# The first table of a two-dimensional transform: loaded in pieces, on three queues, and twelve products of zeros

## Chip, cores and metric

The kernel runs on one core of one Trainium2 chip. The metric is the device time of one execution in microseconds (us), taken from outside the kernel. One core has a matrix engine (PE, with its weight loads listed as PEld), a vector engine (DVE), a scalar engine (ACT), GpSimd (POOL) and a queue-only engine (SP). DMAs are issued from SP, ACT and POOL.

## The reference

Two independent results are computed from 2048 x 576 inputs and set side by side. The first is an attention with 32 heads and a running memory. The second, the one the change is in, is a filter in the frequency domain:

```
X = rfft2(x)            # x is 1 x 2048 x 576
y = irfft2(X * (w_r + 1j*w_i), s=(2048, 576))
out = concatenate([attention(A_x, ...), y], axis=-1)
```

## The kernel before, in words

The program is one long hand-ordered sequence (a manual schedule): the forward transform of the filter, with the weights of the attention loaded beside it; then the projections of the attention, with the middle of the filter beside them; then the inverse transform; then the attention itself. Each engine runs its instructions in the order in which the code emits them.

All large products are done in a split form: an fp32 value is written as a high part in fp32r plus the rest, and high x high, high x low and low x high products are summed in PSUM. An fp32r tile has to be written by something that rounds: ScalarE, VectorE, or a DMA issued from POOL.

The forward transform (`forward`) works on 16 units of 128 sequence positions. For unit u:

- `load(u)` (L114, SP) fetches the rows `xin`, 384 KB, three buffers. `prep(u)` then has VectorE form sum and difference `eo` (L126, two instructions), ScalarE round them to the high part `eh` (L129, L130), and VectorE subtract to get the rest `el` (L133). For units 0 and 1 (`halves`) all this is done for the sum and the difference apart.
- `f1(u)` (L143) is the transform along the 576 columns: 14 products, 7 for each of the two outputs r = 0 (cosines) and r = 1 (sines), with the constant table `tab[:, high or low, r, chunk]` and the short `tab2`.
- `ev0` (L147, ScalarE) and `ev1` (L150, VectorE) take the result from PSUM as high part and rest, `X0` and `X1`.
- `c1(u)` (L163) is the transform along 128 positions: 12 products with the unit's own table `cfw` (`loadc`, L118, POOL), whose blocks are cosine, sine and negated sine, each in high and low. `evz` (L154, ScalarE) stores the result to `Z`.

A loop over u = 0 to 19 emits these in a fixed pipeline. Step u holds, in this order: `ev0(u-1)`, `evz(u-4)`, the first half of `prep(u+2)` (`eo`, `eh`), `ev1(u-1)`, one background instruction of the next stage (`pace`, L208, from step 7 on), the second half of `prep(u+2)` (`el`), `f1(u)`, `load(u+4)`, `c1(u-3)`, `loadc(u+1)`, and a piece of the projection weights (`load_w`: L420 load, L408 ScalarE, L410 VectorE). `prep(0)` and `prep(1)` stand ahead of the loop. So on VectorE a step is: `eo` of unit u+2, `X1` of unit u-1, background, `el` of unit u+2, weights. On ScalarE it is: `X0` of unit u-1, `Z` of unit u-4, `eh` of unit u+2, weights.

Ahead of the loop, POOL fetches the first table in three DMAs (L170: all of the high part, L172: all of the low part, L173: `tab2`) and the first four `cfw`; SP fetches `xin` of units 0 to 2 and the small constants `ident` and `bm` (L404).

Of the kernel before, what the change touches and what calls it, by code (L numbers as in the profile page):

```python
# [5 lines left out]
F32=mybir.dt.float32; F32R=mybir.dt.float32r  # L6
# [19 lines left out]
def tables():  # L26
# [26 lines left out]
    for s2 in range(16):  # L53
        ph=(16*s1*k1+s2*k1)%S
        a=2*np.pi*ph/S
        re=np.cos(a); im=-np.sin(a)
        im[(ph*2)%S==0]=0; re[(ph*4)%S==S]=0; re[(ph*4)%(2*S)==S]=0
        cf.append(np.concatenate([re,im,-im],1))
        ph=ph.T
        re=re.T; im=-im.T  # L60
        ci.append(np.concatenate([-im,re,im],1))
# [1 line left out]
    ci=np.stack(hilo(np.stack(ci)),1).transpose(0,2,1,3)  # L63
    w16=np.zeros((2,9),np.float32)
    return dict(ftab=fwd.reshape(128,-1),ftab2=fwt.reshape(128,-1),itab=inv.reshape(128,-1),itab2=ivt.reshape(128,-1),
                cfw=cf.reshape(16,128,768),civ=ci.reshape(16,128,768))

BORD=[(a,b) for b in range(4) for a in range(4)]

# [33 lines left out]
class FFT:  # L103
# [4 lines left out]
    def forward(s,xp,cp,pp,wl,xs,consts):  # L108
# [6 lines left out]
        def loadc(u):  # L115
            a,b=BORD[u]
            cw[u]=cp.tile([128,2,384],F32R,name="cfw",bufs=4)
            nc.gpsimd.dma_start(cw[u],io["cfw"][4*a+b].rearrange("p (h m) -> p h m",h=2))  # L118
        def prep(u,halves=False):

            x=xin.pop(u)
            eo=xp.tile([128,2,3,128],F32,name="eo",bufs=2)
            h=H[u%3]
            W=(slice(0,1),slice(1,2)) if halves else (slice(0,2),)
            for r,op in enumerate((OP.add,OP.subtract)):
                v.tensor_tensor(eo[:,r],x[:,0],x[:,1],op=op)  # L126
                if halves or r:
                    w=W[r] if halves else W[0]
                    nc.scalar.copy(h[:,w,:2],eo[:,w,:2])  # L129
                    nc.scalar.copy(h[64:97,w,2],eo[64:97,w,2])  # L130
            yield
            l=xp.tile([128,2,3,128],F32R,name="el",bufs=3)
            for w in W: v.tensor_tensor(l[:,w],eo[:,w],h[:,w].bitcast(F32),op=OP.subtract)  # L133
            eh[u],el[u]=h,l
            yield
        def f1(u):
            p=pp.tile([128,2,512],F32,name="f1",tag="f1")
            h,l=eh.pop(u),el.pop(u)
# [24 lines left out]
                        nc.tensor.matmul(p[:,r,:FP],cc[:,hl,k*128:(k+1)*128],x[i][:,q],start=n==0,stop=n==5)  # L163
                        n+=1
        H=[xp.tile([128,2,3,128],F32R,name=f"eh{i}",bufs=1) for i in range(3)]
        for h in H: nc.gpsimd.memset(h[:,:,2].bitcast(F32),0.0)
        load(0)
        tab=cp.tile([128,2,2,2,FP],F32R,name="ftab",bufs=1)
        tab2=cp.tile([128,2,FP],F32R,name="ftab2",bufs=1)
        nc.gpsimd.dma_start(tab[:,0],io["ftab"][:,:4*FP].rearrange("p (r c f) -> p r c f",r=2,c=2))  # L170
        late=consts()
        nc.gpsimd.dma_start(tab[:,1],io["ftab"][:,4*FP:].rearrange("p (r c f) -> p r c f",r=2,c=2))  # L172
        nc.gpsimd.dma_start(tab2,io["ftab2"].rearrange("p (r f) -> p r f",r=2))  # L173
        load(1); load(2); late()
        for u in range(2): loadc(u)
        p=[prep(u,True) for u in range(2)]
        for i in range(2):
            for x in p: next(x)
        load(3)
        s.pace=Pace(61+165+40)  # L180
        for u in range(20):
            p=prep(u+2) if u+2<16 else iter(())
            if 0<u<17: ev0(u-1)
            if 3<u: evz(u-4)
            if u%4==3 and u>6: s.pace.add(s.stage1((u-7)//4))
            next(p,None)
            if 0<u<17: ev1(u-1)
            if u<14: s.pace.take(1)
            next(p,None)
            if u<16: f1(u)  # L190
            if u+4<16: load(u+4)
            elif u<18: next(xs,None)
            if 2<u<19: c1(u-3)
            if 0<u<15: loadc(u+1)
            if 1<u: next(wl,None)
            if u>13: s.pace.take(2)
# [959 lines left out]
```

## Time and profile before

| what | value |
|---|---|
| three runs | 711.28, 709.81, 708.51 us; median 709.81 us |
| the profiled execution, whole | 709.86 us |
| its span, first to last instruction | 708.2 us, so 1.66 us lie around it |
| busy in the span: PE / DVE / ACT / POOL | 678.8 / 544.8 / 455.8 / 194.6 us |
| first wait of PE for the first table | until 9.6 us |
| granted clock of the core | 0.999 |

In the groups and timelines a row gives start, length, engine, line, operation, `out<-in` by the names of the program, shapes, a count, and in square brackets the idle time ahead of it with the engine or DMA that ended it. Products are pipelined, so the pitch from one start to the next says more than the length of one. In a table by stretches the columns are, engine by engine, busy time and number of instructions, then the granted clock of PE, the busy share of the DMA engines, and GB/s.

### The profile page before, as it was taken

To read this page: it belongs to the slowest core of one execution; us is meant where nothing else is said; L and a number is where in the kernel's file an instruction comes from. 1 tells how busy PE (TensorE), PEld (TensorE's weight loads), DVE (VectorE), ACT (ScalarE), POOL (GpSimd) and SP (SyncE) were. 2 spreads that over 40 slices of the span, in tenths; PEclk is the share of its full clock that TensorE was granted. 3 is DMA by queue.
4 is the path that set the end of the run, shared out by engine and by line. 5 is a ranking of instruction groups with operands and counts; after the bars stand their busy time and mean duration, and the time that the engine had idled before them with its cause. 6 is when DMAs were issued, how large, how long until landed. Compare 5 with 4: busy or idle time off the path is not lost.

```text
span 708.2 us, 14408 instructions
## 1 busy us (share of the span) xinstructions
PE 678.8 (96%) x4991; PEld 501.3 (71%) x4991; DVE 544.8 (77%) x1258; ACT 455.8 (64%) x1004; POOL 194.6 (27%) x392
## 2 busy tenths in 40 slices
PE   4999999999999999999999899999999999998997
PEld 3999769879779879998954454445566445663587
DVE  4899969899699789797787787988657876567533
ACT  3777796585686484544388777777656776567421
POOL 3111000100200102665135333444233752235310
PEclk9999999999999999999999999999999999999999
DMA  9897355666384679999338976976766766442151
GB/s 328 256 305 202 115 141 187 186 185 202 100 250 156 178 196 311 202 240 267 100 114 210 190 163 143 207 182 167 154 129 181 182 166 154 92 122 65 29 164 74
DMA packets 71146, 123.80 MB, mean 175 GB/s; under 512 B 12184, under 2 KB 39174, under 8 KB 67482
## 3 DMA queue, kind: packets, MB, share of 16 engines
q1 hardware_dynamic: 64422, 106.89, 57.4%
q0 software_dynamic: 5632, 15.76, 8.2%
q8 instruction: 39, 0.64, 0.4%
q10 hardware_dynamic: 1020, 0.25, 0.2%
q14 instruction: 33, 0.27, 0.1%
HBM read 82.10 MB, written 39.81 MB: 172 GB/s over the span
## 4 chain that ended last, share of the span: by engine, by line
PE 68%; DMA 8%; ACT 4%; DVE 4%; POOL 2%; issue 2%; SPq 0%; ACTq 0%; DVEq 0%; POOLq 0%
PE pj L464 12%; PE pv L734 9%; PE s L656 9%; PE pjv L464 8%; PE po L877 6%; PE i L309 3%; PE i L298 3%; PE s L705 3%; PE s L709 2%; DMA yb<-yout 2%; PE pn L807 2%; PE s L669 2%; PE pm L532 2%; PE s L714 2%; DMA Ks<-qkD 1%
## 5 line engine op out<-in xcount | busy, mean ns | idle before, releaser
L664 DVE CUSTOM_DVE_ANT_0 junk<-s,x 128x512 bf16<-128x512 f32 x248 | 137.0, 552 | 58.0 <-PE s L656 52.6
L719 POOL TENSOR_SCALAR_AFFINE_SELECT P<-P 128x512 f32<-128x512 f32 (+2 forms) x132 | 78.5, 626 | 112.9 <-ACT P L706 104.1
L670 DVE TENSOR_REDUCE mx<-s 128x4 f32<-128x512 f32 x128 | 87.7, 685 | 5.6 <-PE s L669 3.7
L706 ACT ACTIVATE P<-s 128x512 f32<-128x512 f32 x128 | 77.7, 607 | 10.8 <-PE s L705 3.8
L734 PE MATMUL pv<-P,vs 128*32 128x512 f32 (+3 forms) x1024 | 82.5, 439 | 0.1
L715 ACT ACTIVATE P<-s 128x256 f32<-128x256 f32 x128 | 49.8, 389 | 46.1 <-PE s L714 45.7
L711 ACT ACTIVATE P<-s 128x512 f32<-128x512 f32 x128 | 77.4, 605 | 2.4 <-PE s L710 2.2
L656 PE MATMUL s<-Ks,Qs 108*128 108x384 bf16 (+3 forms) x256 | 69.1, 301 | 1.5 <-DMA ux<-uD 1.0
L734 PEld LDWEIGHTS pv<-P,vs 128*32 128x32 f32 x1024 | 26.9, 109 | 45.3 <-issue 35.1
L464 PE MATMUL pj<-x,wqkh 128*128 128x512 f32 x162 | 56.5, 409 | 0.0
L208 DVE TENSOR_TENSOR Z<-t,t 128x290 f32<-128x290 f32 (+1 forms) x96 | 48.4, 553 | 0.1
L656 PEld LDWEIGHTS <-Qs 108*128 108x128 bf16 x320 | 31.5, 98 | 23.5 <-issue 12.1
L208 DVE TENSOR_TENSOR t<-Z 128x580 f32<-128x580 f32 x64 | 46.1, 755 | 0.0
L669 PE MATMUL s<-tri,idb 128*128 128x128 bf16 x256 | 43.0, 219 | 0.0
L522 POOL MEMSET vt<- 128x32 f32 x16 | 2.3, 162 | 141.3 <-PE pm L532 119.5
L298 PE MATMUL i<-civ,Y 128*128 128x256 f32 (+1 forms) x288 | 39.3, 289 | 0.2 <-POOL Y L283 0.2
L298 PEld LDWEIGHTS i<-civ,Y 128*128 128x128 f32 (+1 forms) x288 | 36.5, 181 | 1.0 <-POOL Y L283 0.4
L309 PE MATMUL i<-itab,T 128*128 128x290 f32 (+1 forms) x224 | 36.7, 306 | 0.5 <-DVE yout L317 0.4
L464 PE MATMUL pj<-x,wqkl 128*128 128x512 f32 x90 | 35.6, 395 | 0.0
L464 PE MATMUL pj<-xh,wqkl 128*128 128x512 f32 x90 | 35.5, 395 | 0.0
L143 PE MATMUL f<-ftab,eh 128*128 128x290 f32 x128 | 25.3, 321 | 10.7 <-DMA ftab<-ftab 10.6
L464 PE MATMUL pj<-xh,wqkh 128*128 128x512 f32 x90 | 35.5, 395 | 0.0
(210 smaller groups left out, 1806.3 us busy)
## 6 DMA issues: line engine op xcount, KB each, us to landing
qkD<-sp SPq DMA_DIRECT2D x32, 384.0 KB
xin<-xb SPq DMA_DIRECT2D x16, 384.0 KB
cfw<-cfw POOLq DMA_DIRECT2D x16, 384.0 KB, 4.7
civ<-civ POOLq DMA_DIRECT2D x16, 384.0 KB, 9.0
vs<-vD SPq DMA_DIRECT2D x16, 330.0 KB
vD<-vt SPq DMA_DIRECT2D x16, 311.0 KB
W<-w SPq DMA_DIRECT2D x16, 290.0 KB
yb<-yout SPq DMA_DIRECT2D x16, 290.0 KB
```

Source lines behind the costliest of these rows:

```text
L208: v.tensor_tensor(o,a,b,op=op)
L298: nc.tensor.matmul(p[:m,k],Y[i][:,q,c*128:c*128+m],cc[:,hl,o:o+256],start=n==0,stop=n==5)
L309: nc.tensor.matmul(p,x,t,start=n==0,stop=n==6)
L464: s.nc.tensor.matmul(out,a,b,start=i==0,stop=i==len(L)-1)
L656: nc.tensor.matmul(out,Q[:108,h,128*i:128*i+128],K[:108,h,:128*(i+1)],start=True,stop=True)
L664: nc.vector.tensor_tensor_reduce(out=junk[:,:w],in0=src,in1=s.mask[:,512-w:],scale=1.0,scalar=-3.0e38, op0=OP.add,op1=OP.max,accum_out=s.m ...
L669: nc.tensor.matmul(pa[:,o+w-128:o+w],s.idb,s.tri,start=False,stop=True,skip_group_check=True)
L670: nc.vector.tensor_reduce(out=s.mx[k][:,hh],in_=pa.rearrange("p (b c) -> p b c",c=128),axis=mybir.AxisListType.X,op=OP.max)
L706: nc.scalar.activation(P[0][:,hh],p0,AF.Exp,scale=SC)
L711: nc.scalar.activation(P[1][:,hh],p1,AF.Exp,scale=SC)
L719: nc.gpsimd.affine_select(out=x[:,r],in_=x[:,r],pattern=[[0,r.stop-r.start],[1,128]],compare_op=OP.is_ge,fill=0.0,base=0,channel_multiplie ...
L734: nc.tensor.matmul(s.pvt[32*hh:32*hh+32,128*j:],vt[:,j,19*h:19*h+32],mv[0][:,hh,mv[1]],start=j==0,stop=j>1,skip_group_check=True)
```

## The change

The first table is no longer loaded in three DMAs by POOL alone. It is cut into five pieces of 290 KB. Three of them (high r = 0, low r = 0, high r = 1) go as plain fp32 through the queues of ACT, SP and ACT into buffers of `cfw`, and ScalarE copies them into the fp32r table (`table(n)`, L180 of the changed kernel), between the roundings of the first units. POOL loads `tab2` and low r = 1. `prep` yields after each half, so that the first unit's cosine half is rounded first. The constants `ident` and `bm` move behind `load(3)`. The zeroing of `eh` moves from POOL to VectorE. Twelve products of a tile of zeros are put ahead of the loop on PE; their result is not used. The unit tables `cfw` are stored without the negated third (256 KB in place of 384 KB), and ScalarE makes that block by a copy with scale -1, one instruction per unit, two units before it is used.

```
-        cf.append(np.concatenate([re,im,-im],1))
+        cf.append(np.concatenate([re,im],1))
...
-            nc.gpsimd.dma_start(cw[u],io["cfw"][4*a+b].rearrange("p (h m) -> p h m",h=2))
+            nc.gpsimd.dma_start(cw[u][:,:,:256],io["cfw"][4*a+b].rearrange("p (h m) -> p h m",h=2))
...
-            yield
+                    yield
             l=xp.tile([128,2,3,128],F32R,name="el",bufs=3)
-            for w in W: v.tensor_tensor(l[:,w],eo[:,w],h[:,w].bitcast(F32),op=OP.subtract)
-            eh[u],el[u]=h,l
-            yield
+            for w in W:
+                v.tensor_tensor(l[:,w],eo[:,w],h[:,w].bitcast(F32),op=OP.subtract)
+                eh[u],el[u]=h,l
+                yield
...
-        for h in H: nc.gpsimd.memset(h[:,:,2].bitcast(F32),0.0)
+        z=xp.tile([128,512],BF,name="z",bufs=1)
+        v.memset(z,0.0)
+        for h in H: v.memset(h[:,:,2].bitcast(F32),0.0)
         load(0)
...
-        nc.gpsimd.dma_start(tab[:,0],io["ftab"][:,:4*FP].rearrange("p (r c f) -> p r c f",r=2,c=2))
+        nc.gpsimd.dma_start(tab2,io["ftab2"].rearrange("p (r f) -> p r f",r=2))
+        nc.gpsimd.dma_start(tab[:,1,1],io["ftab"][:,6*FP:].rearrange("p (c f) -> p c f",c=2))
         late=consts()
-        nc.gpsimd.dma_start(tab[:,1],io["ftab"][:,4*FP:].rearrange("p (r c f) -> p r c f",r=2,c=2))
-        nc.gpsimd.dma_start(tab2,io["ftab2"].rearrange("p (r f) -> p r f",r=2))
-        load(1); load(2); late()
+        raw=[]
+        for q,src in ((nc.scalar,io["ftab"][:,:2*FP]),(nc.sync,io["ftab"][:,4*FP:6*FP]),(nc.scalar,io["ftab"][:,2*FP:4*FP])):
+            x=cp.tile([128,2,384],F32,name="raw",tag="cfw",bufs=4)[:,:,:FP]; raw.append(x)
+            q.dma_start(x,src.rearrange("p (c f) -> p c f",c=2))
+        def table(n): nc.scalar.copy((tab[:,0,0],tab[:,1,0],tab[:,0,1])[n],raw[n])
+        load(1); load(2)
         for u in range(2): loadc(u)
         p=[prep(u,True) for u in range(2)]
-        for i in range(2):
-            for x in p: next(x)
-        load(3)
+        table(0); next(p[0]); table(1); next(p[0]); next(p[0]); table(2); next(p[0])
+        for x in p[1]: pass
+        load(3); late()
+        p=pp.tile([128,2,512],F32,name="c1",tag="c1")
+        for i in range(12): nc.tensor.matmul(p[:,0],z[:,:128],z,start=True,stop=True)
         s.pace=Pace(61+165+40)
         for u in range(20):
             p=prep(u+2) if u+2<16 else iter(())
             if 0<u<17: ev0(u-1)
             if 3<u: evz(u-4)
+            if 1<u<18: nc.scalar.activation(cw[u-2][:,:,256:],cw[u-2][:,:,128:256].bitcast(F32),AF.Copy,scale=-1.0)
```

The first place at which the order of instructions moves is the start of ScalarE's program (eh_112, eh_113 and eh_114 are the buffers of units 0, 1 and 2). Before:

```order
L129 ACT_TABLE_LOAD
L129 CAST eh_112<-eo 128x256
L130 CAST eh_112<-eo 33x128
L129 CAST eh_112<-eo 128x256
L130 CAST eh_112<-eo 33x128
L129 CAST eh_113<-eo 128x256
L130 CAST eh_113<-eo 33x128
```

With the change, on the same engine at the same place:

```order
L179 DMA raw<-ftab 128x2x290 x2
L180 ACT_TABLE_LOAD
L180 CAST ftab<-raw 128x580
L129 CAST eh_112<-eo 128x256
L130 CAST eh_112<-eo 33x128
L180 CAST ftab<-raw 128x580
L129 CAST eh_112<-eo 128x256
L130 CAST eh_112<-eo 33x128
L180 CAST ftab<-raw 128x580
L129 CAST eh_113<-eo 128x256
```

Two DMA issues and three copies now stand there, and unit 1's first rounding stands behind the third copy.

The second place is the start of SP's queue. Before, the three first units, the two small constants, and the fourth unit and those after it:

```order
L114 DMA xin<-xb 128x768 x3
L404 DMA ident<-ident 128x128
L404 DMA bm<-bm 126x133
L114 DMA xin<-xb 128x768 x4
L420 DMA raw<-wqk 128x576
```

With the change:

```order
L114 DMA xin<-xb 128x768
L179 DMA raw<-ftab 128x2x290
L114 DMA xin<-xb 128x768 x3
L414 DMA ident<-ident 128x128
L414 DMA bm<-bm 126x133
L114 DMA xin<-xb 128x768 x3
L430 DMA raw<-wqk 128x576
```

A piece of the table now stands between units 0 and 1, and the constants behind unit 3.

The third place is one step of the loop on ScalarE, u = 4: X of unit 3, Z of unit 0, the rounding of unit 6 and a piece of the weights. Before:

```order
L147 CAST X_293<-f_259 128x580
L154 COPY Z<-c_276 128x580
L129 CAST eh_112<-eo 128x2x256
L130 CAST eh_112<-eo 33x2x128
L408 CAST wqkh<-raw 128x576
```

With the change:

```order
L148 CAST X_318<-f_284 128x580
L155 COPY Z<-c_301 128x580
L194 ACTIVATE cfw<-cfw 128x2x128
L129 CAST eh_112<-eo 128x2x256
L130 CAST eh_112<-eo 33x2x128
L418 CAST wqkh<-raw 128x576
```

The negation stands ahead of the rounding that VectorE's `el` waits for.

2 lines of the change are left out of this document (1 added, 1 removed).

## The prediction

> **What bounds the kernel.** I read the page first, then the waits of PE, then the start of the program and the loop of the forward transform engine by engine.
>
> ```profile
> span 708.2 us, 14408 instructions
> PE   4999999999999999999999899999999999998997
> ```
>
> PE is busy nearly throughout; the one slice with a large hole is the first. The longest of PE's waits (total, times, longest):
>
> ```profile
> PE f L143 <- DMA ftab<-ftab: 10.6, 2, 9.6
> ```
>
> So 10.6 us of PE's time go to the first table, and one would expect a gain of several us. But an earlier start of PE is worth only what the engines that feed it can follow. The busy table by stretches (PE, PEld, DVE, ACT, POOL, clock, DMA share, GB/s):
>
> ```profile
> 0.00:5.00 5.00, 0.00 (x0) 0.00 (x0) 1.02 (x2) 1.69 (x2) 4.39 (x16) 1.00 0.57 198
> 5.00:10.00 5.00, 0.38 (x1) 0.41 (x2) 3.69 (x9) 2.39 (x7) 0.99 (x2) 1.00 1.05 343
> 35.00:40.00 5.00, 5.00 (x39) 5.00 (x38) 5.00 (x10) 3.07 (x7) 0.53 (x1) 1.00 0.96 322
> 50.00:55.00 5.00, 4.97 (x37) 4.73 (x36) 5.00 (x10) 3.14 (x6) 0.53 (x1) 1.00 0.88 266
> ```
>
> From 35 us on VectorE is busy all the time, and PE later gets through 37 products in 5 us where it had 39. The starts of units 9 and 10 on PE, and a line of the waits after 15 us:
>
> ```profile
> 40.73 0.69 PE L143 MATMUL f<-ftab,eh 128*128 128x290 f32 x4
> ...
> 44.35 0.81 PE L143 MATMUL f<-ftab,eh 128*128 128x290 f32 x4
> ```
>
> ```profile
> PEld f L143 <- DVE X L150: 1.2, 5, 0.3
> ```
>
> Unit 10 starts 3.62 us after unit 9, and five times PE waits for VectorE's X1, which frees the PSUM of `f1`. So the end of the forward transform hangs on VectorE's chain. That chain itself:
>
> ```profile
> 9.32 1.03 DVE L126 TENSOR_TENSOR eo<-xin 128x384 f32<-128x384 f32 x2 [1.18 <-DMA xin<-xb]
> 11.45 0.96 DVE L133 TENSOR_TENSOR el<-eo,eh 128x768 fp32r<-128x768 f32 x1 [1.11 <-ACT eh L130]
> 13.62 1.03 DVE L126 TENSOR_TENSOR eo<-xin 128x384 f32<-128x384 f32 x2 [1.21 <-DMA xin<-xb]
> 15.68 0.76 DVE L150 TENSOR_TENSOR X<-f,X 128x580 fp32r<-128x580 f32 x1 [1.03 <-ACT X L147]
> 16.75 0.96 DVE L133 TENSOR_TENSOR el<-eo,eh 128x768 fp32r<-128x768 f32 x1 [0.31 <-ACT eh L130]
> 17.63 1.02 DVE L126 TENSOR_TENSOR eo<-xin 128x384 f32<-128x384 f32 x2
> ...
> 20.70 1.02 DVE L126 TENSOR_TENSOR eo<-xin 128x384 f32<-128x384 f32 x2
> ...
> 43.54 0.75 DVE L150 TENSOR_TENSOR X<-f,X 128x580 fp32r<-128x580 f32 x1
> ```
>
> From unit 4's `eo` at 17.63 no step of it waits for PE or a DMA any more: it is 3.07 us to unit 5's, and on to 43.54 there is only the turn through ScalarE's rounding inside a step. The row at 43.54 is the X1 behind which PE starts unit 10 at 44.35. **Whatever the change does at the start counts by what it does to 17.63**, not by when PE begins. Behind the forward transform PE's digits are 9 nearly everywhere, so no gap would take up a shift; I carry a shift to the end whole.
>
> **The change part by part.** First, when does unit 4's `eo` come? Before, it hung on the first table: ScalarE's X of unit 0 waited for PE, and the rounding of unit 3 stood behind it.
>
> ```profile
> 4.58 0.41 ACT L129 CAST eh<-eo 128x256 fp32r<-128x256 f32 x1 [2.48 <-DVE eo L126]
> 5.01 0.29 ACT L130 CAST eh<-eo 33x128 fp32r<-33x128 f32 x1
> ...
> 15.01 0.64 ACT L147 CAST X<-f 128x580 fp32r<-128x580 f32 x1 [3.59 <-PE f L143]
> 15.67 0.62 ACT L129 CAST eh<-eo 128x512 fp32r<-128x512 f32 x1
> ```
>
> That wait goes, since unit 0's products will be through before unit 3's `eo`. What is late next is the arrival of unit 1: a piece of the table now stands ahead of it on SP, and two more run beside it on ACT's queue. From unit 1's landing the chain is: one `eo` half, 0.55; two pairs of roundings, 0.75 each (0.43 to the second, 0.29 for it and a hop); the last `el` half, 0.5, so 2.55 to unit 2's `eo`. From there 3.0 to unit 3's (2.13 from 9.32 to `el`, and 0.88 from an `el` to the next `eo`, as from 16.75 to 17.63), then one step of 3.07. Sum 8.6. ScalarE's third copy (0.64 by the 580 wide cast) runs while unit 1's `eo` is formed, if its piece lands no later than unit 1. So nothing is gained or lost if **unit 1 lands at 17.63 - 8.6 = 9.0 us**. Unit 3's own landing, 13.62 before, does not bind: two of the four unit tables no longer run ahead of it, and it has until 14.6.
>
> When does unit 1 land? Two stretches of the DMA view (1 to 2 and 2 to 3 us), the sizes, and the first uses:
>
> ```profile
> DMA packets 8, 0.02 MB, mean 25 GB/s; under 512 B 0, under 2 KB 0, under 8 KB 8
> DMA packets 94, 0.29 MB, mean 289 GB/s; under 512 B 0, under 2 KB 0, under 8 KB 94
> ```
>
> ```profile
> xin<-xb SPq DMA_DIRECT2D x16, 384.0 KB
> ftab<-ftab POOLq DMA_DIRECT2D x2, 580.0 KB, 8.2
> ```
>
> ```profile
> 3.98 2.15 DVE L126 TENSOR_TENSOR eo<-xin 128x384 f32<-128x384 f32 x4 [3.98 <-DMA xin<-xb]
> ...
> 9.62 0.82 PE L143 MATMUL f<-ftab,eh 128*128 128x290 f32 x2 [9.62 <-DMA ftab<-ftab]
> ```
>
> A unit is 0.393 MB and a piece, a quarter of 1160 KB, 0.297 MB. By 5 us 0.99 MB have come (198 GB/s), then 343 GB/s. Units 0 and 1 with the three plain pieces are 1.68 MB, there at 7.0 us; with POOL's two pieces all ahead, 2.27 MB, 8.7 us; with one of them 7.9. What is moved is usable later: unit 0's 0.393 MB are through at 3.3 us and used at 3.98, 0.7 later; three units and the first half of the table, 1.77 MB, are through at 7.3 and used at 9.62, 2.3 later. Bounds for unit 1: 7.7 and 11.0. I take 7.9 and 1.2, so 9.1: half of POOL's pieces, and a lag nearer to that of the same queue and size. **The start costs 0.1 us, with a gain of 1.3 and a loss of 2.0 as its ends.**
>
> The Trainium skill, DMA: Bandwidth & Descriptors, section Issuing engines are not separate DMA queues, speaks against the change: DMAs started by scalar, sync and gpsimd run on the same 16 engines and interleave. By that rule all 2.27 MB share the way, unit 1 would come at the late end, and the sum would be 711.9. The DMA share of 1.05 from 5 to 10 us agrees that no engine was spare there.
>
> Second, the twelve zero products and the earlier first product. The early products run at about half pace, though the clock column says 1.00:
>
> ```profile
> 13.07 1.17 PE L143 MATMUL f<-ftab,eh 128*128 128x290 f32 x4
> 14.04 0.93 PE L143 MATMUL f<-ftab,el 128*128 128x290 f32 x3
> ...
> 17.72 0.71 PE L143 MATMUL f<-ftab,eh 128*128 128x290 f32 x4
> 18.27 0.57 PE L143 MATMUL f<-ftab,el 128*128 128x290 f32 x3
> ```
>
> Four products take 0.97 us from start to start at 13.07 and 0.55 at 17.72, so 0.24 and 0.14 each; the 28 products of units 0 and 1 at the fast pace would save at most 2.8 us. That is under cover: VectorE wants units 0 and 1 only after unit 3's `eo`. I count 0, with 2.8 as the bound on the gain. The zero products themselves run in PE's empty first 9 us and cost nothing.
>
> The Trainium skill, TensorE: Matmul & The Clock Gate, Part 1, says that the array starts at half clock, is released by some 3.4 us of activity, and falls back after as long an idle stretch. The two pitches agree with it, the clock column does not show it; by the rule the zero products would buy 2.8 us on PE, a sum of 707.1 if PE set the end.
>
> Third, the negation on ScalarE: one 128 x 256 instruction per unit, 0.43 from start to start by the rounding at 4.58. It stands ahead of `eh`, where ScalarE idles:
>
> ```profile
> 39.89 0.62 ACT L129 CAST eh<-eo 128x512 fp32r<-128x512 f32 x1 [0.98 <-DVE eo L126]
> ```
>
> 0.98 us hide 0.43; I count 0. Without that cover each of the ten steps 4 to 13, those with a weight piece, would cost 0.43. For the last two units, whose products follow without an `f1` between, I count 0 too, with 0.43 each as the bound.
>
> Fourth, 128 KB less per unit table, 2.1 MB in all: the waits after 15 us name no DMA in the forward transform's loop, so 0 either way. The table loads of units 1 to 3 now wait for ScalarE's copies; behind them POOL has only further unit tables, used past 21 us. The zeroing on VectorE falls into its idle 3.98 us; the moved constants are used after the forward transform: 0.
>
> **Sum:** 709.86 (the span of 708.2 and 1.66 around it) + 0.1 = **710.0 us**; the profiled execution lies at the median of the three runs, 709.81.
>
> **Rivals.** (a) PE's start sets the end after all: then unit 2, at 17.72 on PE before, starts when its `el` is ready, 5.5 us behind unit 1's landing, at 14.6: 3.1 us gained, 706.7, and 705.5 if the five waits for X1 (1.2 us) go too. For it speaks the first slice of PE; against it, the row at 44.35. (b) Slower by transfers: unit 1 lands at 11.0, because POOL's and ACT's pieces share the DMA engines with SP and come through first; this decides from 9.0 us on, and its 2.0 us give 711.9. (c) Slower by the negation: if it waits for its table, or takes over 0.9 us, `eh` comes late in ten steps, and 0.43 each gives 714.2. Against it stands the idle 0.98. (d) The zero products do not speed PE up: then the 2.8 us stay, under cover, and it is 710.0 all the same, so (d) shares my forecast's chance.
>
> **How the numbers follow.** Forecast 0.55, (a) 0.16, (b) 0.18, (c) 0.11. The range goes down to 706.7 by (a), and up to 711.9 by (b) and 0.7 for the scatter between the runs, 712.6; left out are (c) and the far end of (a), some 0.19. Half a per cent is 3.5 us, about what a measurement of this kernel can tell from no change: faster than 706.3 is two thirds of (a), 0.10; slower than 713.4 nearly all of (c), 0.10; the rest is 0.80.
>
> **What would show it.** Right: unit 1's `eo` on VectorE at about 9 us, unit 4's at 17 to 18, the X1 ahead of unit 10 near 43.5, PE waiting for X1 from an earlier unit than 10, while PE's own first products come several us earlier and at 0.14. Wrong: unit 4's `eo` more than 2 us from 17.63; the idle time ahead of `eh` gone; products waiting for a negation; or a shift at 44.35 that doesn't arrive at the end.

## The result, and the profile after

| | before | with the change |
|---|---|---|
| median of the runs beside each other (22 each) | 709.59 us (706.68 to 713.31) | 711.76 us (709.25 to 716.56) |
| the profiled execution, whole / its span | 709.86 / 708.2 us | 711.22 / 709.5 us |
| granted clock of the profiled execution | 0.999 | 0.991 |

The ratio is 1.0036, with a 95% interval of 1.0023 to 1.0049, that is 2.6 us slower (1.6 to 3.5); the medians lie 2.2 us apart. 710.0 was forecast with a range of 706.7 to 712.6, so the time lies inside the range, and less than half a per cent from before, but the 0.1 us of the forecast is too little by about 2. The upper part of the range stood for a late landing of unit 1, which did not happen; that the time falls into it has other causes, which follow.

The head of the page of the changed kernel (span, and the slices of PE):

```profile
span 709.5 us, 14451 instructions
PE   7999999999999999999999999999999999998987
```

PE's first slice is busy to 7 tenths where it was 4, the zero products among them, as the change was meant to do. Nothing came of it. The start of VectorE shows the forecast chain, row by row:

```profile
8.68 1.03 DVE L126 TENSOR_TENSOR eo<-xin 128x384 f32<-128x384 f32 x2 [0.54 <-DMA xin<-xb]
...
14.61 1.02 DVE L126 TENSOR_TENSOR eo<-xin 128x384 f32<-128x384 f32 x2
15.54 0.76 DVE L151 TENSOR_TENSOR X<-f,X 128x580 fp32r<-128x580 f32 x1
16.80 0.96 DVE L134 TENSOR_TENSOR el<-eo,eh 128x768 fp32r<-128x768 f32 x1 [0.50 <-ACT eh L130]
17.67 1.02 DVE L126 TENSOR_TENSOR eo<-xin 128x384 f32<-128x384 f32 x2
```

Unit 1 is there for VectorE at 8.68 (9.1 was taken) and unit 4's `eo` comes at 17.67, against 17.63 before and a forecast of 17.7. PE on the other hand starts 3.6 us earlier (6.00 in place of 9.62) and has nothing left of it a few units on:

```profile
1.26 5.30 PE L188 MATMUL c<-z 128*128 128x512 bf16 x12 [1.26 <-DVE z L168]
6.00 1.51 PE L144 MATMUL f<-ftab,eh 128*128 128x290 f32 x4
...
8.51 0.40 PE L144 MATMUL f<-ftab,el 99*128 99x290 f32 x1 [0.74 <-DMA ftab<-ftab]
9.77 1.46 PE L144 MATMUL f<-ftab,eh 128*128 128x290 f32 x4 [0.86 <-ACT ftab L180]
...
16.35 0.81 PE L144 MATMUL f<-ftab,eh 128*128 128x290 f32 x4 [1.68 <-DVE X L151]
...
17.62 1.17 PE L144 MATMUL f<-ftab,eh 128*128 128x290 f32 x4
18.59 0.93 PE L144 MATMUL f<-ftab,el 128*128 128x290 f32 x3
...
21.91 1.79 PE L164 MATMUL c<-X,cfw 128*128 128x290 f32 x12
```

It waits for `tab2`, the short table that POOL loads (by the order of the program the product at 8.51 is the one that reads it; the trace leaves the number off the name), for ScalarE's copy of the third plain piece, and for unit 0's `X1` (the 15.54 on VectorE), and behind these waits its clock is at half again: four products take 0.97 us from 17.62 to 18.59. Now the clock column shows it (table by stretches, with the columns of the prediction):

```profile
10.00:13.60 3.60, 3.54 (x15) 3.30 (x15) 2.06 (x4) 1.94 (x6) 0.71 (x1) 0.54 1.29 362
...
17.00:20.40 3.40, 3.40 (x16) 3.14 (x15) 2.90 (x5) 2.42 (x5) 0.00 (x0) 0.52 0.70 223
```

The mean clocks of the two traces, 0.999 and 0.991, do not measure what the change lost here: before, units 0 and 1 ran at the same half pace (0.24 a product) while the column said 1.00.

The first c1 starts at 21.91, and unit 11 on PE at 48.33 where it was 48.16: the forward transform is as it was, within 0.2 us. Behind it stands a wait that the forecast did not have. The first product of the projections, before and with the change:

```profile
71.57 0.63 PE L464 MATMUL pj<-x,wqkh 128*128 128x512 f32 x2
```

```profile
72.63 0.74 PE L474 MATMUL pj<-x,wqkh 128*128 128x512 f32 x2 [0.73 <-ACT Z L155]
```

The product waits for the evacuation of unit 15's `Z` by ScalarE (71.93 to 72.57), and starts 1.06 us later than before. Before there is no wait. So three questions were open: where this wait comes from, where the rest of the loss comes from, and why 3.6 us on PE are worth nothing.

### The profile page after: what moved, and what is told of

Read it like the earlier page. It is cut to its first block, busy times and chain, and to the rows that moved or that the text cites. A ratio compares the mean times of both kernels' runs of the same rounds, so it can differ in the third digit from the quotient of the medians.

```text
span 709.5 us, 14451 instructions
## 1 busy us (share of the span) xinstructions
PE 685.9 (97%) x5003; PEld 505.1 (71%) x5003; DVE 546.3 (77%) x1262; ACT 462.4 (65%) x1023; POOL 195.5 (28%) x388
## 5 line engine op out<-in xcount | busy, mean ns | idle before, releaser
L680 DVE TENSOR_REDUCE mx<-s 128x4 f32<-128x512 f32 x128 | 87.7, 685 | 5.2 <-PE s L679 3.3
L474 PEld LDWEIGHTS pj<-x,wqkh 128*128 128x128 f32 x162 | 30.4, 188 | 8.2 <-ACT Z L155 1.0
```

The source lines that it names most:

```text
L474: s.nc.tensor.matmul(out,a,b,start=i==0,stop=i==len(L)-1)
L680: nc.vector.tensor_reduce(out=s.mx[k][:,hh],in_=pa.rearrange("p (b c) -> p b c",c=128),axis=mybir.AxisListType.X,op=OP.max)
```

## The experiments

All twelve ran in five rounds beside the kernel before. The table gives for each what the readings below use: unit 4's `eo` on VectorE, the first product of unit 2 on PE, the first projection product, and the ratio to the kernel before.

| kernel | unit 4's `eo` | unit 2 on PE | first projection | ratio (95%) |
|---|---|---|---|---|
| before | 17.63 | 17.72 | 71.57 | |
| the change | 17.67 | 16.35 | 72.63 | 1.0036 (1.0023 to 1.0049) |
| e1_again | 17.46 | 16.14 | 72.54 | 1.0032 (1.0014 to 1.0051) |
| e2_f1bank | 17.38 | 16.05 | 71.31 | 1.0021 (1.0004 to 1.0038) |
| e3_no_neg | 17.41 | 16.09 | 72.23 | 1.0026 (1.0008 to 1.0043) |
| e4_chain | 17.73 | 18.10 | 72.41 | 1.0033 (1.0011 to 1.0054) |
| e5_before | 17.04 | 16.97 | 70.99 | 1.0001 (0.9980 to 1.0023) |
| e6_no_zero | 17.70 | 16.38 | 71.64 | 1.0012 (0.9991 to 1.0033) |
| e7_ahead | 15.70 | 17.54 | 73.03 | 1.0036 (1.0017 to 1.0055) |
| e8_before_ahead | 17.59 | 19.43 | 74.08 | 1.0057 (1.0035 to 1.0079) |
| e9_short | 17.59 | 14.22 | 67.59 | 0.9989 (0.9964 to 1.0015) |
| e10_before_short | 20.46 | 17.41 | 70.30 | 1.0028 (1.0003 to 1.0053) |
| e11_delay | 17.37 | 16.83 | 74.85 | 1.0040 (1.0020 to 1.0060) |
| e12_short_no_neg | 17.87 | 14.51 | 67.61 | 0.9960 (0.9941 to 0.9980) |

### The new wait, and the rest

The theory: the twelve zero products write a tile of `c1`, which is thereby the first to ask for PSUM, where before `f1` was; so `c1` sits in the banks that the first projection tile is given later, and that tile has to wait until the last `c1` is evacuated. The rivals: the negation makes ScalarE late with `Z`; or the times of the change are a chance of the late part of the kernel.

**e1_again**: the changed kernel as it is.

> The changed kernel once more, nothing altered, for a second trace. Placement theory: the zero products' tile is the first to ask for PSUM under the tag of c1, so c1 gets the banks that the first projection product is given later, and that product waits for the evacuation of unit 15's Z; so again a first projection product about 1 us later than before (72.6 against 71.6 us), put to ScalarE's Z, and unit 4's eo near 17.7. Negation theory: the same row, since it is the same kernel. If the profiled half-clock stretch near 683 us is chance, it does not come back or comes elsewhere, and the time lies 1.5 to 2.5 us over before; if it belongs to the change, it is there again.

The wait is there again, with the same 0.73, and the projections start at 72.54. The ratio agrees. What differs between the two traces of the change lies late: the first loses about 2 us near 683 us, the second as much near 400, each in a stretch of lower clock behind a wait of PE (0.73 over the stretch from 684 to 688 us, and 0.63 from 400 to 404).

**e2_f1bank**: the zero products get a tile of `f1`.

```
-        p=pp.tile([128,2,512],F32,name="c1",tag="c1")
+        p=pp.tile([128,2,512],F32,name="f1",tag="f1")
         for i in range(12): nc.tensor.matmul(p[:,0],z[:,:128],z,start=True,stop=True)
```

> The changed kernel with one edit: the zero products write a tile of the tag of f1, not of c1, so that f1 asks for PSUM first, as it did before the change. Placement theory: the wait of the first projection product for ScalarE's Z is gone and it starts near 71.7 us, 0.9 earlier than in the changed kernel; the whole is 0.7 to 1 us faster than the changed kernel. Negation theory (the copies with scale -1 push the last evacuations of Z back): the wait stays, first projection product at 72.6. Both: unit 4's eo at 17.7, as nothing at the start changes.

```profile
71.31 0.63 PE L474 MATMUL pj<-x,wqkh 128*128 128x512 f32 x2
```

The wait is gone and the projections start 1.3 us earlier than with the change. One name in one line did it. The traces do not show where a tile lies, but the programs built from these kernels do, and they agree: with the change unit 15's `c1` and the first projection tile both get bank 0 of PSUM, one of the parts into which it is divided; before, and with the tile named `f1`, unit 15's `c1` lies in bank 6 and the first projection tile in bank 0.

**e3_no_neg**: the full unit tables and no negation, the zero products as in the change.

```
-        cf.append(np.concatenate([re,im],1))
+        cf.append(np.concatenate([re,im,-im],1))
...
-            nc.gpsimd.dma_start(cw[u][:,:,:256],io["cfw"][4*a+b].rearrange("p (h m) -> p h m",h=2))
+            nc.gpsimd.dma_start(cw[u],io["cfw"][4*a+b].rearrange("p (h m) -> p h m",h=2))
...
-            if 1<u<18: nc.scalar.activation(cw[u-2][:,:,256:],cw[u-2][:,:,128:256].bitcast(F32),AF.Copy,scale=-1.0)
```

> The changed kernel with the unit tables loaded whole (384 KB with the negated third) and without the sixteen negations on ScalarE; pieces, zero products and their tile stay. Placement theory: the first projection product still waits for Z of unit 15, which is bound by its own products, and starts within 0.2 us of 72.6. Negation theory: the wait falls by 0.4 us or more, or goes. If the negations cost time anywhere else in the loop, unit 11 starts on PE earlier than 48.3 us; I expect 48.2 to 48.4, since they lie in idle time of ScalarE, or later by up to 0.5 if the larger tables push unit 1's landing back.

```profile
72.23 0.73 PE L473 MATMUL pj<-x,wqkh 128*128 128x512 f32 x2 [0.73 <-ACT Z L155]
```

The wait stays at 0.73 without any negation: that rival falls. What the negation itself costs is seen on ScalarE in the step at 23 to 25 us, with the change and then without the negation:

```profile
23.52 0.64 ACT L148 CAST X<-f 128x580 fp32r<-128x580 f32 x1 [0.62 <-PE c L164]
...
24.73 0.42 ACT L194 ACTIVATE cfw<-cfw 128x256 fp32r<-128x256 f32 x1
25.05 0.61 ACT L129 CAST eh<-eo 128x512 fp32r<-128x512 f32 x1
```

```profile
23.43 0.65 ACT L148 CAST X<-f 128x580 fp32r<-128x580 f32 x1 [0.80 <-PE c L164]
...
24.64 0.62 ACT L129 CAST eh<-eo 128x512 fp32r<-128x512 f32 x1
```

In this one step the idle time ahead of `eh` is used up, and the rounding comes at 25.05 where it could have come at 24.73, 0.3 us late at most; `el` behind it waits 0.62 in place of 0.50, so 0.1 us reaches VectorE. In the steps around it idle time is left ahead of `eh` (0.91 and 0.23 in this trace), and the negation is hidden as forecast.

**e6_no_zero**: the change without the zero products and their tile.

```
-        z=xp.tile([128,512],BF,name="z",bufs=1)
-        v.memset(z,0.0)
...
-        p=pp.tile([128,2,512],F32,name="c1",tag="c1")
-        for i in range(12): nc.tensor.matmul(p[:,0],z[:,:128],z,start=True,stop=True)
```

> The change without its twelve zero products and their tile, everything else kept. Theory 1 (the zero products buy nothing under VectorE's chain, and the wait of the first projection product for the evacuation of unit 15 comes from the tile which they take first): units 0 and 1 run at half pace, but unit 4's eo still comes at 17.4 to 17.7 and unit 11 within 0.3 us of 48.2; the first projection product has no wait of 0.73 and starts at 71.3 to 71.8 where the change had 72.6; the time is about 1 us under that of the change, 710.8. Rival (the zero products keep PE's clock up and that is worth something): unit 11 comes later than in the change by 0.5 us or more, and the time is as in the change or above it, 711.8 to 713.

```profile
16.38 0.81 PE L144 MATMUL f<-ftab,eh 128*128 128x290 f32 x4 [1.36 <-DVE X L151]
...
19.45 0.80 PE L144 MATMUL f<-ftab,eh 128*128 128x290 f32 x4 [0.91 <-DVE X L151]
```

Unit 2 comes at 16.38 where the zero products had it at 16.35: they buy nothing, and the idle time that they could have saved is spent waiting for VectorE's `X1`, here at unit 3 too. e2_f1bank shows the same from the other side. There the clock stayed full (1.00 from 5.0 to 15.4 us), PE was through units 0 and 1 at 12.88, and then it waited for the same `X1`:

```profile
12.31 0.57 PE L144 MATMUL f<-ftab,el 128*128 128x290 f32 x3
16.05 1.33 PE L144 MATMUL f<-ftab,eh 128*128 128x290 f32 x4 [3.18 <-DVE X L151]
```

In e6_no_zero the wait for `Z` is gone (71.64). The ratio, 1.0012, is the lowest of the changed kernels that keep the order of the forward transform, though its interval overlaps those of the others.

**e5_before**: the kernel before against itself.

> The kernel before, unchanged, against itself. The ratio should be 1.000 within 0.002, which says how far the 1.0036 and 1.0032 of the change can be chance. The two traces of the change each had one stretch of half clock late in the kernel (at 682.7 and at 399.5 us, 1.6 to 2.9 us each), and the one trace of before had none. Theory 1, it is chance that any kernel of this length meets: this trace may show one too, and the times scatter as those of the change do. Theory 2, the change brings it: this trace shows none, the granted clock stays near 0.999, and the drift of the two traces of before against each other from 75 us on stays under 0.5 us until 680 us. In the forward transform unit 4's first VectorE instruction should come at 17.6 and the last unit's product at 65.1, both within 0.2, since nothing there differs.

The ratio is 1.0001. The trace says how much two executions of one and the same kernel differ. Here unit 4's `eo` comes at 17.04, 0.6 us before the first trace's (0.2 at most had been expected), there is no stretch of half clock ahead of its last 3 us, and at 464 us PE waits where it did not wait in the first trace. First this kernel, then the first trace of before:

```profile
464.54 0.38 PE L854 MATMUL pb<-rr,sel 96*72 96x512 bf16 x1 [1.44 <-DMA rr<-rrD]
```

```profile
463.05 0.41 PE L854 MATMUL pb<-rr,sel 96*72 96x512 bf16 x1
```

0.6 us ahead at 71 us, this execution is 1.5 behind at 464, and level at the end. So a drift of 2 us behind 75 us is ordinary, and a single trace can't tell whose it is.

What follows for the sum: at the first projection product the two traces of before stand at 71.28 on the mean, the two of the change at 72.59, the two without a `c1` tile for the zero products (e2, e6) at 71.48. That is a loss of 1.3 us, and 0.9 of it is the wait that this tile brings: from the start of the last 48 products of `c1` to the first projection product it is 7.33 us in the change, e1 and e3, and 6.44 in both traces of before, in e2 and in e6. The other 0.4 lies in the forward transform, no more than two executions of the kernel before differ by there. At VectorE's first `mx` (L670 before, L680 with the change), near 293 us, the traces of the change still stand 0.9 and 0.7 us behind the first of before (293.83 and 293.66 against 292.95), so nothing is added up to there. The traces thus account for 1.3 of the 2.3 to 2.6 us by the ratios of e1 and of the result. The missing 1 us is **not settled**: 1.3 lies inside the interval of the one (1.0 to 3.6 us) and 0.3 below that of the other, and two executions of the kernel before drift by more than 1 us.

### Why PE's earlier start earns nothing

Theory A is the prediction's: VectorE's chain of `eo` and `el` alone sets the end of the forward transform. Theory B: what counts is where `X1` stands in VectorE's order. `X1` of unit 0 frees the PSUM that unit 2's `f1` needs; it stands behind unit 3's `eo`, so PE can't use an early start, and a PE that is late makes `X` late in its turn.

**e4_chain**: ScalarE rounds units 0 and 1 ahead of the three table copies; SP fetches units 0 to 2 first, and all three pieces go through ACT's queue; the zero products in a tile of `f1`.

```
-        load(0)
+        load(0); load(1); load(2)
...
-        for q,src in ((nc.scalar,io["ftab"][:,:2*FP]),(nc.sync,io["ftab"][:,4*FP:6*FP]),(nc.scalar,io["ftab"][:,2*FP:4*FP])):
+        for q,src in ((nc.scalar,io["ftab"][:,:2*FP]),(nc.scalar,io["ftab"][:,4*FP:6*FP]),(nc.scalar,io["ftab"][:,2*FP:4*FP])):
...
-        table(0); next(p[0]); table(1); next(p[0]); next(p[0]); table(2); next(p[0])
-        for x in p[1]: pass
+        for x in p:
+            for _ in x: pass
+        for n in range(3): table(n)
```

> The changed kernel with the tile of the zero products under the tag of f1, and the start ordered for VectorE's chain: SP fetches units 0, 1 and 2 before anything else, all three plain pieces of the table go by ACT's queue, and ScalarE rounds units 0 and 1 before it copies the three pieces. Theory of the prediction (what counts is when unit 4's eo starts on VectorE, not when PE starts): unit 4's eo at 15.0 to 16.5 instead of 17.7, although PE's first product of the table comes later (8 to 9 us instead of 6.0), and unit 11 starts on PE as much earlier, 46 to 47 instead of 48.3; with the placement undone as well the whole is 2 to 3 us faster than the changed kernel and about 1 us faster than before. Rival (PE's start sets the end): unit 11 at 48.3 or later, the whole not faster than the run with the placement alone.

A miss. Unit 1's `eo` came at 6.89, but the copies, whose pieces now land late, stand ahead of unit 2's rounding on ScalarE, so unit 4's `eo` is at 17.73 again; and PE, waiting for the copies, starts unit 2 only at 18.10. The edit moved the wait from one place to the other, so neither forecast was put to the test. One thing in it speaks against theory A all the same: unit 4's `eo` stands where e6_no_zero has it (17.73 and 17.70) and no projection waits for `Z`, yet the projections start 0.8 us later (72.41 against 71.64). Unit 5's `eo` comes 3.54 us behind unit 4's in place of 3.06, since the late PE makes `X` of unit 1 late.

**e7_ahead**: on e2_f1bank, `eo` of each unit is formed one step earlier, ahead of the `el` of the unit before it; `X0` of unit 0 ahead of unit 2's rounding; four `eh` and two `xin` buffers. The heart of the edit (the buffers, the order of the loads and the steps ahead of the loop are left out):

```
-            p=prep(u+2) if u+2<16 else iter(())
+            p,ahead=ahead,prep(u+3) if u+3<16 else iter(())
...
-            next(p,None)
+            next(ahead,None)
             if 0<u<17: ev1(u-1)
             if u<14: s.pace.take(1)
             next(p,None)
```

> The change with the zero products in a tile of f1, and VectorE's chain loosened: the sum and difference of each unit are formed one step earlier, ahead of the rest of the unit before, so that VectorE no longer waits for ScalarE's rounding inside a step; X of unit 0 is taken before the rounding of unit 2; four buffers of eh, two of xin. Theory 1 (VectorE's chain sets the forward transform's end; PE's earlier start is worth something only when that chain lets it): unit 4's eo comes at 14.5 to 16, PE's early start now counts, units 2 and later start 1.5 to 3 us earlier than in the change, VectorE's steps shrink from 3.07 to about 2.8, PE waits for X1 no more or rarely, unit 11 at 45.5 to 47 where it was 48.2, and the time falls by 1.5 to 3 us against the kernel before, 706.5 to 708.5. Rival (the end of the forward transform hangs on something else, as the weights' loads or the background work): unit 11 within 0.5 us of 48.2 though eo comes early, and the time as with the zero products' tile alone, 710.8.

Another miss, and the one that taught most. VectorE and PE of this kernel:

```profile
15.70 1.03 DVE L126 TENSOR_TENSOR eo<-xin 128x384 f32<-128x384 f32 x2 [0.34 <-DMA xin<-xb]
16.64 0.75 DVE L151 TENSOR_TENSOR X<-f,X 128x580 fp32r<-128x580 f32 x1
```

```profile
17.54 1.31 PE L144 MATMUL f<-ftab,eh 128*128 128x290 f32 x4 [5.00 <-ACT eh L129]
...
23.42 1.77 PE L164 MATMUL c<-X,cfw 128*128 128x290 f32 x12
```

Unit 4's `eo` comes 2.0 us earlier than with the change, and the projections 0.4 later. `X1` of unit 0 now stands behind unit 4's `eo`, which waits for its DMA, and ends at 17.39; PE idles for 5.0 us and starts unit 2 right behind it, 1.2 us later than with the change, and at half pace. (The row names ScalarE's `eh`, but by the order of the program the `X1` that ended at 17.39 is what was late.) Theory A is refuted as it stands: when `eo` comes does not set the end by itself. Both theories had been mixed up in my expectation, since I counted PE's start as free once `eo` was early.

**e8_before_ahead**: the same edit on the kernel before.

> The same loosening of VectorE's chain on the kernel before: its table loads, its order of the first units and its full unit tables kept, no zero products. Theory 1 (with the chain loosened PE's start becomes the bound): PE begins at 9.6 as before and its units 0 and 1 run at half pace, so unit 2 on PE stays at 17.4 to 17.8 and the first c1 at 21.3 to 21.6; only the waits for X1 later on go, unit 11 comes 0.3 to 1.2 us earlier than 48.2, and the time is 0.3 to 1.2 us under the kernel before, 708.3 to 709.3, that is 1 to 2 us above the same edit on the change. Rival (the chain alone counts and the table never did): unit 11 comes as early as in the same edit on the change, within 0.3 us, and the two times agree.

Unit 2 on PE comes at 19.43, 1.7 us later than before, by the same mechanism, and the projections 2.5 us later; a gain of 0.3 to 1.2 had been expected. The same edit on the change stands 1.05 us better (73.03 against 74.08), so there the early table is worth something.

**e9_short**: on e2_f1bank, `X` of unit u is taken in step u in place of u + 1, so that `X1` falls into the gap in which VectorE waits for ScalarE's rounding; c1, Z and the negation one step earlier. `eo`, `el`, the loads and the table are untouched.

```
-            if 0<u<17: ev0(u-1)
-            if 3<u: evz(u-4)
-            if 1<u<18: nc.scalar.activation(cw[u-2][:,:,256:],cw[u-2][:,:,128:256].bitcast(F32),AF.Copy,scale=-1.0)
+            if u<16: f1(u); ev0(u)
+            if 2<u<19: evz(u-3)
+            if 0<u<17: nc.scalar.activation(cw[u-1][:,:,256:],cw[u-1][:,:,128:256].bitcast(F32),AF.Copy,scale=-1.0)
...
-            if 0<u<17: ev1(u-1)
+            if u<16: ev1(u)
...
-            if u<16: f1(u)
...
-            if 2<u<19: c1(u-3)
+            if 1<u<18: c1(u-2)
```

> The change with the zero products in a tile of f1, and X of unit u taken in step u in place of step u+1 (X0 ahead of the rounding of unit u+2, X1 in the gap in which VectorE waits for that rounding), c1 two steps behind f1 in place of three, Z and the negation one step earlier. VectorE's order of eo and el, the loads and the table are as they were. Theory A (VectorE's eo and el chain alone sets the end, as the prediction had it): unit 4's eo stays at 17.3 to 17.8 and unit 11 and the last c1 move by less than 0.5 us. Theory B (two chains of about the same length run side by side, VectorE's eo and el, and PE's f1 that waits for X1 to free its PSUM; a late PE is passed on as a late X in the next step): unit 2 on PE starts at 14 to 15 in place of 16.35, the first c1 at 18.5 to 20 in place of 21.9, VectorE's waits for ScalarE's rounding shrink, and since PE's 14 + 12 products take 3.5 us a unit and VectorE's step 3.6, unit 11 comes 1 to 2 us before 48.2 and the time is 707.5 to 709, 1 to 2 us under the kernel before.

```profile
11.50 1.02 DVE L126 TENSOR_TENSOR eo<-xin 128x384 f32<-128x384 f32 x2
12.44 0.76 DVE L151 TENSOR_TENSOR X<-f,X 128x580 fp32r<-128x580 f32 x1
13.63 0.96 DVE L134 TENSOR_TENSOR el<-eo,eh 128x768 fp32r<-128x768 f32 x1 [0.44 <-ACT eh L130]
...
17.59 1.02 DVE L126 TENSOR_TENSOR eo<-xin 128x384 f32<-128x384 f32 x2
```

```profile
14.22 0.71 PE L144 MATMUL f<-ftab,eh 128*128 128x290 f32 x4
...
16.13 1.78 PE L164 MATMUL c<-X,cfw 128*128 128x290 f32 x12
```

This decides for theory B. Unit 4's `eo` has not moved (17.59), `X1` of unit 0 comes at 12.44 in place of 15.54, unit 2 on PE at 14.22 in place of 16.35, and the projections start at 67.59, 4.0 us ahead of the kernel before and 5.0 ahead of the change. VectorE's own chain has not moved, here or later: unit 15's `eo` comes at 57.92 beside 57.87 before, and the `X1` behind it at the same time too, first before, then here:

```profile
58.80 0.75 DVE L150 TENSOR_TENSOR X<-f,X 128x580 fp32r<-128x580 f32 x1
```

```profile
58.85 0.74 DVE L151 TENSOR_TENSOR X<-f,X 128x580 fp32r<-128x580 f32 x1
```

What the edit changed is whose `X1` that is: unit 13's in place of unit 12's. So VectorE's chain still sets the times, and the order decides which unit gets them: the gain is about one step. But of the 4.0 us little reaches the end: 709.24 us beside 709.39. The profile shows where the first half goes. PE and ScalarE at the first product of the next kind:

```profile
77.63 0.38 PE L502 MATMUL pj<-sp,nid 128*128 128x512 bf16 x1 [1.71 <-ACT sp L500]
```

```profile
75.77 0.67 ACT L228 ACTIVATE tw<-Z 128x580 f32<-128x580 f32 x1
76.35 0.75 ACT L417 CAST wvh<-raw 128x288 fp32r<-128x288 f32 x2
77.00 0.57 ACT L500 CAST sp<-pj 128x512 bf16<-128x512 f32 x1
```

Ahead of the `sp` that PE needs, ScalarE has the background of the filter's middle and the next weights, which is bound to the steps and not to time, and `sp` comes only 1.9 us earlier than before (77.00 against 78.90); that gives back 1.9 us. In this execution more than the rest went at 286 and 466 us, in two long waits of PE (3.52 and 1.75 us) with lower clock behind them; the first:

```profile
282.00:286.00 4.00, 0.48 (x4) 0.28 (x3) 3.97 (x5) 1.41 (x4) 3.83 (x6) 1.00 0.71 177
286.00:290.00 4.00, 4.00 (x22) 4.00 (x23) 2.03 (x4) 1.69 (x4) 0.25 (x2) 0.57 0.41 111
```

**e10_before_short**: the same shorter pipeline on the kernel before.

> The same shorter pipeline on the kernel before, with its table in three DMAs and no zero products. Theory B: X0 of unit 0 now stands on ScalarE ahead of the rounding of unit 2, and waits for PE's first products, which wait for the table until 9.6 and run at half pace to about 13.6; so the rounding of unit 2 falls from 10.4 to 14.5 or later, unit 2 on PE starts at 17.5 to 18.5, unit 4's eo comes 2 to 4 us later than 17.6, and the time is 0.5 to 3 us above the kernel before: what the early table of the change is worth shows only when something waits for unit 0's products. Theory A: the time follows unit 4's eo whole, so 2 to 4 us above. Rival: the table's time is no part of it, and this kernel gains as much as the same edit on the change, 1 to 2 us.

```profile
15.44 0.76 DVE L150 TENSOR_TENSOR X<-f,X 128x580 fp32r<-128x580 f32 x1 [5.35 <-ACT X L147]
...
17.38 1.02 DVE L126 TENSOR_TENSOR eo<-xin 128x384 f32<-128x384 f32 x2
```

Unit 2's step waits 5.35 us for unit 0's products, as expected, and the time is 2.0 us over the kernel before by the ratio (0.2 to 3.8). Two details were off: the 17.38 in the last row is unit 3's `eo` (unit 4's comes at 20.46, 2.8 late), and the projections start at 70.30, 1.3 us early all the same; the wait for `sp` takes 1.7 of that back at 80 us. Against the same edit on the change the projections are 2.7 us later: **this is what the early table is worth, once something can use it**. It rests on one trace of each kernel, and the zero products come with the early table here; the smaller unit tables and the negation have no part in it (e12). It goes by way of VectorE: unit 4's `eo` is 2.87 us apart in the two kernels.

**e11_delay**: the kernel before, with the sum and difference of unit 8 formed four times.

```
-                v.tensor_tensor(eo[:,r],x[:,0],x[:,1],op=op)
+                for _ in range(4 if u==8 else 1): v.tensor_tensor(eo[:,r],x[:,0],x[:,1],op=op)
```

> The kernel before, with the sum and the difference of unit 8 formed four times in place of once: six more instructions on VectorE, 3.1 us by its row of 1.03 for two, in the step at 30 us in which it is nearly always busy. Nothing else is changed. It asks two things at once. Is VectorE's chain really what PE waits for in the middle of the forward transform? If so unit 11 on PE comes 2.5 to 3.1 us later than in the kernel before; if PE's own chain has the room, less than 1.5. And is a shift at 68 us carried to the end? If the prediction's rule holds for a loss, the time is 2.5 to 3.1 us above the kernel before, 712 to 712.7; if what follows takes up a shift in both directions, as it took up half of the 4 us gained with the shorter pipeline, 1 to 1.6.

```profile
30.97 4.58 DVE L126 TENSOR_TENSOR eo<-xin 128x384 f32<-128x384 f32 x8
35.46 0.75 DVE L150 TENSOR_TENSOR X<-f,X 128x580 fp32r<-128x580 f32 x1
```

```profile
36.27 1.33 PE L143 MATMUL f<-ftab,eh 128*128 128x290 f32 x4 [2.83 <-DVE X L150]
```

The eight take 4.58 us where two take 1.02, so this step takes VectorE 3.6 us more, not 3.1. PE waits 2.83 for the `X1` behind them and then runs at half pace. The projections start 3.28 us later than before, products at 330 us are 3.31 later, and the time is 2.8 us over by the ratio (1.4 to 4.3), 4.1 by the medians. A loss is carried to the end whole, as far as these times can tell.

**e12_short_no_neg**: the shorter pipeline of e9, with full unit tables and no negation.

Against e9_short, beside the table lines of e3_no_neg:

```
-            if 0<u<17: nc.scalar.activation(cw[u-1][:,:,256:],cw[u-1][:,:,128:256].bitcast(F32),AF.Copy,scale=-1.0)
```

> The shorter pipeline on the change with the zero products in a tile of f1, and now also with the full unit tables of 384 KB and no negation on ScalarE. Theory B holds if unit 2 starts on PE at 14 to 14.6 again, the first c1 by 16.5, and the projections start 3.5 to 4.5 us before 71.6; half of that is given back at the first store of keys at 77.6, where ScalarE and VectorE have background work left over. With 0.43 less on ScalarE for each unit there is a little less left over. The time is 706.5 to 709.5, 0 to 3 us under the kernel before, and the ratio within 0.002 of that of the same pipeline with the negation. If ScalarE's negation mattered in the shorter pipeline, the projections start over 1 us earlier than there. The long waits of PE at 282 and 466 us, each followed by half clock in the trace of that kernel, should be gone if they are chance, and be there again if the earlier start of the projections brings them.

707.90 us beside 709.28, ratio 0.9960 (0.9941 to 0.9980): faster than the kernel before, and so than the change, by a little. The projections start where e9's do (67.61 and 67.59), so the negation takes nothing from the forward transform in this order either. The wait for `sp` is there again, 1.59 us at 77.53. It leaves a lead of 2.2 us at 80 us, and that is about what is found at the end: 1.4 us between the medians, 2.8 by the ratio (1.4 to 4.2). The two long waits of e9's trace are not in this one, so the earlier projections don't bring them by themselves; whether the smaller tables have a part in them was not tried. Between e9 and e12 the ratios do not decide, since their intervals overlap.

## Why the prediction was right or wrong, point by point

- **The start costs 0.1 us.** Right in size: unit 1 at 8.68 (9.1 taken), the chain of 8.6 us from there as summed, plus 0.4 in its first part, unit 4's `eo` at 17.67, unit 11 0.17 later than before. That the 17.7 is met to a few hundredths is luck: the landing came 0.4 early and the chain took 0.4 longer. e1 to e3 give 17.38 to 17.46, and before itself 17.04 in its second trace, so the start of either kernel is known to half a microsecond only. Rival (b), unit 1 at 11.0, did not come.
- **"Whatever the change does at the start counts by what it does to 17.63, not by when PE begins."** Right within one order of VectorE's instructions, and too narrow as a reason. While the order is fixed, `eo` and `X1` move together: so before and with the change, and so in e9 and e10, where `eo` is 2.87 us apart and the projections 2.71. But PE waits for `X1` and not for `eo`. e7 put `eo` 2.0 us earlier and lost; e9 left it and moved the projections 4 us forward by taking each `X1` one step earlier; and in e4 a late PE made the steps behind unit 4 late, which the forecast had not allowed for. Rival (a), unit 2 on PE at 14.6, did not come (16.35), though e9's order brings it to 14.22: there PE's early start is worth about 2.7 us (against e10).
- **"The zero products themselves run in PE's empty first 9 us and cost nothing."** This is the step that failed. Their time is free, and they buy nothing (e6: unit 2 at 16.38 and 16.35 without and with them), but the tile that they write changes which PSUM banks `c1` has, and the first projection product waits 0.73 us for `Z`, 0.9 us later in all (7.33 us behind the last products of `c1` in place of 6.44; e2 and e6 against the change). I had priced the instructions and not the buffer.
- **The bound of 2.8 us for the clock.** Not reached in the change, where the clock fell back behind the waits for the table's pieces (0.74 and 0.86) and for `X1` (1.68): 0.54 from 10.0 to 13.6 us and 0.52 from 17.0 to 20.4. But the cover that was forecast is what counts: in e2 the clock stayed full over units 0 and 1, and PE spent the time in a longer wait for `X1` (3.18).
- **The negation is hidden.** Right but for one step (0.1 us on VectorE). Rival (c) did not come.
- **A shift is carried whole to the end.** Right for a loss (e11: 3.28 at the projections, 3.31 at 330 us). Wrong for a gain: of 4.0 us, 2.2 are left at 80 us (e12), because ScalarE's background ahead of `sp` is done only 1.9 us earlier (e9).
- **PE would wait for `X1` from an earlier unit than 10.** It waits at unit 2 (1.68) and for 0.26 at unit 3, but then not again until unit 11: a unit takes PE 3.52 us in between, VectorE's step is 3.07 us at first, which puts PE behind, and 3.7 to 3.9 from unit 6 on, which lets PE catch up.
- **About 1 us** of the 2.3 to 2.6 was found in no wait that belongs to the change, as said above.

## What to carry to other kernels

An early start of an engine is worth what the instruction that frees its next buffer allows: look for that instruction's place in the order of its engine, not only for the engine that is busy. A tile that is written once for nothing still takes part in the placement of all that come after it, so price the buffer with the instructions, and look at the first use of the space in the next stage. A gain at one stage is to be followed through the next, whose background work may be bound to steps; the one loss tried here went through whole.

## What was not expected of the hardware

PE's clock can fall to half in the trace after much shorter waits than I had thought. In e11_delay PE waits 2.83 us at 33 us, in a stretch where it is otherwise busy:

```profile
32.00:36.00 4.00, 1.44 (x11) 1.20 (x9) 3.83 (x8) 0.37 (x1) 0.53 (x1) 1.00 0.71 225
36.00:40.00 4.00, 3.73 (x17) 3.73 (x18) 3.51 (x7) 3.03 (x6) 0.00 (x0) 0.57 0.51 152
```

A mean of 0.57 over 4 us is 3.4 us at half. In the change the waits of 0.74 and 0.86, both between 7.8 and 9.8 us, were followed by a fall, and at 680 us a wait of 1.47 with one of 0.43 behind it, where the clock is 0.73 from 684 to 688 us:

```profile
680.87 0.38 PE L896 MATMUL pb<-rr,sel 96*126 96x512 bf16 x1 [1.47 <-DVE ux L897]
...
682.61 1.26 PE L887 MATMUL po<-woh,oh 126*128 126x288 f32 x4 [0.43 <-ACT ob L889]
```

Not every such wait brings a fall. In e5_before the wait of 1.44 us ahead of 464.54 leaves the clock at 1.00 from 464 to 468 us, in e6_no_zero those of 1.36 and 0.91 leave it at 1.00 from 15 to 21 us, and in e2_f1bank three of 0.48, 0.79 and 0.60 between 6.3 and 9.5 us leave it at 1.00. So the length of one wait does not decide it, and what does is not settled here.

The Trainium skill, TensorE: Matmul & The Clock Gate, Part 1, puts the fall at an idle window of some 3.4 us. The length of the half stretches agrees with that window; the waits ahead of them here are shorter than it, and the measurement decides. 3.4 us at half pace lose up to 1.7 us beside the wait itself, which is most of the 2 us by which the two traces of the change jump at 400 and 683 us.
